# A recurrence and a highway layer from a hand-written list of operations: halves of output products for the last units, and a new list

## The chip, the cores and the metric

The kernel runs on one core of one Trainium2 chip. The metric is device time in microseconds. The engines are called as in the profile: PE (TensorE, matrix products and transposes), PEld (its weight loads), DVE (VectorE), ACT (ScalarE), POOL (GpSimd) and SP (the queue that issues the transfers). PSUM is the memory that PE writes to and from which DVE and ACT read.

## The reference

Two layers in a row over four sequences of 6336 tokens with 256 features. The first is a gated recurrence along the tokens, the second a highway layer with two 256 x 256 weight matrices. All inputs and the output are float32.

```python
f = lower_bound + (1 - lower_bound) * sigmoid(f_logit)
h = f[:, t] * h + (1 - f[:, t]) * x[:, t]          # for each token t; y[:, t] = h
H = maximum(y @ w_h, 0)
T = sigmoid(y @ w_t + b_t)
out = T * H + (1 - T) * y
```

## The kernel before, in words

The 25344 tokens are cut into 28 units: units 0 and 1 of 2 blocks of 128 tokens, unit 2 of 4, units 3 to 25 of 8, unit 26 of 4, unit 27 of 2. Each unit goes through the same stages, and most stages have two parts, one for each half of the 256 features (or of the unit's tokens). A part is a token of a list that is written out by hand as a string, such as `z23.0:0`: the letter says the stage, 23 is the unit, 0 the part, and the number behind the colon is the buffer (slot) that the result takes. A `v` at the end puts the work on DVE where another engine is the default. The stages:

- `l`, `x` (line 237, SP): load the logits and the inputs, 1 MB each for a full unit. `wt`, `wh` load the weights.
- `u` (line 249, ACT): sigmoid of the negated logits. `b` (line 257, POOL, `v` DVE): bv = u * x.
- `i` (line 264, PE): transposes u, features on partitions. `f` (line 275 ACT, line 273 DVE with `v`): the gate f from it.
- `p` (line 284, PE): transposes bv. `s` (line 301, DVE): the scan along the tokens, y; it needs the last column of the unit before.
- `z`, `g` (lines 114 and 313, PE): products of both halves of y with w_t and w_h. `t` (line 326, ACT): sigmoid of z. `d` (line 330, DVE): max of -(1 - lower_bound) * y and g, by which the rectified part minus y comes out. `e` (line 336, POOL, `v` DVE): d = d * t.
- `o` (lines 355 and 356, PE): sums y and d back to token order in PSUM, four blocks of 128 tokens at a time. `c` (line 368 ACT, line 366 DVE with `v`): copy to SBUF. `w` (line 372, SP): store, 512 KB for four blocks.
- `k` (lines 125 and 114, PE): `k*3` is three products of zeros that keep PE working.

PSUM has eight banks. Slots 0, 1 and 2 of `z`, `g`, `o` and `k` hold two banks each (`two_banks`, line 134); slots `a0` and `a1` are one bank each, and shared with the transposes `i` and `p`. A PE operation that takes a slot waits until its last reader is done.

The program keeps the order of the list on every engine: each engine's queue is the list with the other engines' tokens left out, and an engine never passes a waiting operation. The SP queue holds loads and stores in list order too, so a load behind a store waits for that store's copy. One more rule: a POOL product waits for the last DVE product of the same kind listed ahead of it (`shared`, line 178).

`part` (line 341) says how many blocks an `o` and its `c` cover, and a store waits for all copies of its four blocks:

Of the kernel before, what the change touches and what calls it, by code (L numbers as in the profile page):

```python
# [53 lines left out]
s3.1:0 c1.0:1 w1.0 x6:1 b4.1:1 l7:0 z2.0:2 p3.0:1 i4.0:0 t2.1:0 g2.0:0 s3.0 g2.1:1 d2.0:0 b4.0 x27:2 t2.0 k*3:2 f4.0:0
x7:3 e2.0 d2.1 e2.1 i4.1:0 u5:1 p4.0:1 f4.1:1 z3.0:0 b5.1:0 z3.1:1 t3.0:1 b5.0 t3.1 p4.1:0 k*3:2 s4.0:1 u6:0 u27:2
s4.1 g3.1:0 g3.0:1 i5.1:1 d3.1:1 f5.1:0 i5.0:0 e3.2 l8:2 o2.0:2 d3.0 e3.0v c2.0:0 f5.0:1 g4.1:0 e3.1v x8:5 i6.1:1
b6.1:1 g4.0:1 d4.1:0 d4.0 f6.1:2 o3.0:2 i6.0:0 p5.0:1 s5.0:2 o3.1:0 c3.0:1 f6.0:3 c3.1:2 b6.0 z4.0:1 w3.1 w3.0 p5.1:0
w2.0 z4.1:2 k*3:0 l9:1 s5.1 p6.0:1 u7:1 t4.1:0 x9:0 t4.0 s6.0:0 b27.0:2 l11:0 k*3:0 b7.0:0 x11:1 z5.0:0 l10:3 x10:2
t5.0:1 p6.1:0 g5.1:2 b7.1 e4.1 s6.1 z5.1:1 i7.0:1 d5.1:1 u8:0 f7.0:0 t5.1 k*3:0 g5.0:0 d5.0 i8.1:0 i7.1:1 b8.1:1
z6.0:2 e4.0v e4.2v f8.1:1 f7.1:2 p7.0:0 g6.0:0 e5.0v e5.2v e5.1v t6.0:0 i8.0:1 f8.0:3 b8.0 o4.1:1 d6.0:2 o5.0:2 e6.0  # L60
c4.1:0 p7.1:1 u9:1 c5.0:1 k*3:0 s7.0:3 o4.0:0 w5.0 c4.0:2 w4.1 b9.1:0 w4.0 z6.1:1 b9.0 t6.1 i9.0:0 g6.1:2 s7.1 f9.0v:0
d6.1 l12:1 z7.1:0 i9.1:1 p8.1:0 s8.1:1 e6.1 u11:0 f9.1:2 g7.1:1 k*3:2 t7.1:1 e6.2 i11.1:1 p8.0:0 x12:3 b11.1:3 o5.1:0
l13:2 d7.1:0 s8.0 f11.1:1 g7.0:1 z7.0:2 u10:1 i10.1:1 c5.1:3 b11.0 p9.0:0 t7.0 d7.0 s9.0:2 f10.1:3 o6.0:0 b10.1:1
g8.1:1 w5.1 b10.0 i10.0:1 c6.0:1 f10.0:0 z8.0:2 p9.1:0 d8.1:1 o6.1:0 t8.0:0 c6.1:0 w6.1 u12:1 e7.0 g8.0:1 p10.0:1
x13:0 s9.1 d8.0 z8.1:2 i11.0:0 z9.0:0 k*3:1 f11.0:2 t9.0:2 b12.1:0 l14:0 s10.0:0 t8.1 p10.1:0 s10.1 o7.0:1 c7.0:2
u13:0 w7.0 g9.1:0 p11.1:1 x14:1 l17:1 g9.0:2 w6.0 d9.1:2 l15:3 i12.0:0 o7.1:1 f12.0:0 c7.1:0 d9.0 z10.1:0 z10.0:2
p11.0:0 t10.1:1 z9.1:1 t10.0 s11.1:3 g10.0:0 w7.1 s11.0 i12.1:1 g10.1:2 e8.0 t9.1 x15:2 d10.0:0 d10.1 f12.1:1 b12.0
o8.1:1 i13.1:0 u14:1 f13.1:2 b13.1:1 o8.0:0 c8.1:2 p12.1:1 b13.0 z11.1:2 i13.0:0 t11.1:0 c8.0:3 e9.0v e10.0 g11.1:1
# [5 lines left out]
b16.1 g14.1:0 i16.0:0 t13.1 f16.0:2 e13.0 b17.1:3 s15.0:3 z14.1:1 t14.1:1 o12.0:2 p15.1:0 g14.0:1 d14.1:1 b17.0
c12.0:2 w12.0 p16.0:1 u18:3 s15.1 z14.0:0 t14.0 x19:0 d14.0 o12.1:2 e14.0 c12.1:3 i16.1:0 f16.1:1 z15.0:1 t15.0:0
g15.1:0 o13.0:2 w12.1 c13.0:0 b18.0:0 s16.0:1 p16.1:0 d15.1:2 w13.0 l20:1 i17.1:1 l21:2 x20:1 g15.0:0 s16.1 b18.1
o13.1:1 f17.1:2 d15.0 p17.0:1 p17.1:0 u19:0 s17.1:2 c13.1:1 z16.1:2 t16.1:2 s17.0 z15.1:0 w13.1 o14.0:1 t15.1 z16.0:2
i18.0:0 g16.1:0 c14.0:2 g16.0:1 i18.1:1 w14.0 t16.0 f18.0:1 o14.1:2 f18.1:0 d16.1:0 d16.0 z17.0:0 c14.1:0 x21:3 w14.1
# [5 lines left out]
t19.1:1 t19.0 g19.1:1 b22.0 d19.1 i21.0:0 w17.0 g20.1:0 d20.1:1 o18.0:2 p21.0:1 f21.0:2 u23:1 s21.0:2 p21.1:0 o18.1:1
z20.0:0 c18.0:2 l24:0 e19.0 g20.0:2 c18.1:0 w18.0 i22.1:1 z20.1:1 s21.1 t20.0:0 o19.1:0 f22.1:2 b23.0:1 x24:0 d20.0
p22.1:0 s22.1:0 t20.1 c19.1:3 i23.1:1 o19.0:1 g21.1:0 f23.1:0 d21.1:0 i23.0:1 c19.0:1 p22.0:0 b23.1 g21.0:1 w18.1
u24:0 f23.0:2 s22.0 d21.0 z21.0:0 t21.0:1 z21.1:2 i24.0:1 f24.0:1 t21.1 p23.1:0 s23.1:3 z22.1:0 g22.1:1 w19.1 i24.1:1
# [2 lines left out]
l26:2 o21.0:0 w20.1 c21.1:2 i25.0:1 g23.0:2 i25.1:0 c21.0:3 f25.0:0 b25.0 d23.0 f25.1:1 g24.1:0 z24.0:1 u26:0 i27.1:0  # L90
p25.0:1 z23.1:2 e22.0 f27.1:2 e22.2 x26:0 d24.1:0 o22.0:0 e23.0 p25.1:0 s25.0:2 t24.0:1 o22.1:1 w20.0 s25.1 t23.1
z24.1:2 c22.0:0 g24.0:0 c22.1:1 d24.0 e23.2 i26.0:1 g25.0:1 d25.0:2 t24.1 i27.0:0 b26.1:0 g25.1:2 f26.0:0 f27.0:1
d25.1 i26.1:1 b26.0 z25.0:0 w21.1 f26.1:3 p26.1:0 o23.1:1 s26.1:0 t25.0:2 e23.1 p26.0:1 e24.0 s26.0 o23.0:2 p27.1:0
# [4 lines left out]
"""

    NU = len(units)  # L100
# [57 lines left out]
    cc = sb([P, NH], FP32, "cc")  # L158
# [180 lines left out]
        return q * 4, min(q * 4 + 4, units[n][0])  # L339

    def part(n, k):
        w = 2 if n in () else 4
        return k * w, min(k * w + w, units[n][0])

    def do_o(n, k, eng, slot):
        op = two_banks(slot, "op").rearrange("p (j d) -> p j d", d=D)
        a, c = part(n, k)
        j0, j1 = blocks(n, a // 4)
        g = j1 - j0
        for j in range(a, c):  # L350
            lo = j0 * P + j - j0
            cols = slice(lo, lo + g * (P - 1) + 1, g)
            for h in range(NH):
                o = op[:, j - a, h * P:(h + 1) * P]
# [1 line left out]
                pin(nc.tensor.matmul(o, half(n, "d", h)[:, cols], ident_b, start=False, stop=True))  # L356
        st[n]["op", k] = op

    def do_c(n, k, eng, slot):
        a, c = part(n, k)  # L360
# [4 lines left out]
        if eng:
            pin(nc.vector.tensor_copy(to, of))
        else:
            pin(nc.scalar.copy(to, of))  # L368
# [44 lines left out]
```

## Time and profile before

| what | us |
| --- | --- |
| median of three runs | 208.80 |
| lowest and highest run | 208.68, 209.03 |
| the profiled execution | 208.92 |
| its span, first to last instruction | 207.1 |
| PE, DVE, ACT, POOL busy | 196.7, 193.0, 191.8, 176.9 |

The profile lists busy times for each engine, groups of equal instructions with a count, a mean in ns and the idle time ahead of them with what ended it, and stretches of the span. In rows of a timeline the first number is the start, the second the duration, and a bracket gives the idle time of the engine just before it and what ended it. The granted clock of PE was 0.994 of full speed over the span.

### The profile page before, as it was taken

The page shows a single profiled execution, that of the slowest core. Times are in us where ns is not written, and L with a number is a line of the kernel's source. Part 1 is how long each engine was busy: PE and PEld are TensorE (multiplying, and loading weights), DVE is VectorE, ACT ScalarE, POOL GpSimd, SP SyncE. Part 2 cuts the span into 40 slices and gives each one's busy share as a digit, 9 for nine tenths or more (in the row PEclk, how much of TensorE's full clock was granted, in tenths as well). Part 3 has the DMA queues.
Part 4 walks back from the last instruction along what each step waited for, and adds up shares of the span by engine and source line. Part 5 has one row for each costly group of instructions (what it writes and reads, how often), then busy time and mean ns, then how long its engine had stood idle before and what let it go on. Part 6 is the DMA issues. An engine that isn't in the chain of part 4 may idle for free.

```text
span 207.1 us, 4655 instructions
## 1 busy us (share of the span) xinstructions
PE 196.7 (95%) x1835; PEld 136.3 (66%) x1864; DVE 193.0 (93%) x157; ACT 191.8 (93%) x187; POOL 176.9 (85%) x94
## 2 busy tenths in 40 slices
...
GB/s 194 386 426 419 419 416 418 415 401 426 419 414 418 422 430 416 413 421 394 354 418 420 415 418 426 415 422 422 422 426 415 323 422 370 337 136 203 186 297 279
DMA packets 15980, 78.67 MB, mean 380 GB/s; under 512 B 1748, under 2 KB 2264, under 8 KB 10072
## 3 DMA queue, kind: packets, MB, share of 16 engines
...
q14 instruction: 6, 0.05, 0.1%
q10 hardware_dynamic: 8, 0.00, 0.0%
...
## 4 chain that ended last, share of the span: by engine, by line
PE 71%; DVE 10%; DMA 9%; issue 3%; ACT 2%; POOL 2%; SPq 0%; ACTq 0%; DVEq 0%; POOLq 0%
PE z L313 9%; PE g L313 9%; PE op L356 9%; PE op L355 9%; PE bT L284 9%; PE uT L264 8%; PE g L114 8%; PE z L114 7%; DVE y L301 7%; DMA x<-in_x_dram 7%; DMA l<-in_f_logit_dram 2%; DVE d L330 2%; POOL bv L257 2%; PE idle L114 1%; DVE d L336 1%
## 5 line engine op out<-in xcount | busy, mean ns | idle before, releaser
L257 POOL TENSOR_TENSOR bv<-u,x 128x1024 bf16<-128x1024 f16 (+1 forms) x51 | 103.1, 2049 | 14.1 <-DVE d L336 6.0
L301 DVE TENSOR_TENSOR_SCAN y<-f,y,bT 128x1024 bf16<-128x1024 f16 (+5 forms) x54 | 106.2, 1989 | 0.3 <-PE bT L284 0.2
L336 POOL TENSOR_TENSOR d<-d,t 128x512 bf16<-128x512 bf16 (+3 forms) x32 | 74.0, 2322 | 10.7 <-DVE d L336 4.1
L330 DVE SCALAR_TENSOR_TENSOR d<-y,ncc,g 128x1024 bf16<-128x1024 bf16 (+2 forms) x56 | 62.8, 1139 | 2.2 <-PE g L313 2.1
L326 ACT ACTIVATE t<-z,bt 128x1024 bf16<-128x1024 f32 (+2 forms) x56 | 57.3, 1058 | 1.6 <-PE z L313 1.0
L275 ACT ACTIVATE f<-uT,ncc 128x1024 f16<-128x1024 f16 (+2 forms) x51 | 53.8, 1065 | 2.7 <-PE uT L264 2.2
L249 ACT ACTIVATE u<-l 128x2048 f16<-128x2048 f32 (+2 forms) x28 | 48.9, 1753 | 4.8 <-DMA l<-in_f_logit_dram 4.8
L368 ACT COPY o<-op 128x1024 f32<-128x1024 f32 (+1 forms) x50 | 50.8, 1027 | 1.9 <-PE op L356 1.6
L355 PE MATMUL op<-diag,y 128*128 128x128 f16 x396 | 49.8, 219 | 0.8 <-DVE d L330 0.6
L356 PE MATMUL op<-ident_b,d 128*128 128x128 bf16 x396 | 49.5, 219 | 0.2 <-DVE d L336 0.2
L356 PEld LDWEIGHTS <-d 128*128 128x128 bf16 x396 | 44.0, 113 | 5.2 <-DVE d L336 1.1
L355 PEld LDWEIGHTS <-y 128*128 128x128 bf16 x396 | 44.2, 113 | 3.1
L313 PE MATMUL g<-y,w_sb 128*128 128x512 bf16 (+1 forms) x111 | 39.1, 367 | 1.0 <-ACT t L326 0.2
L313 PE MATMUL z<-y,w_sb 128*128 128x512 bf16 (+1 forms) x108 | 38.0, 367 | 0.7
L264 PEld LDWEIGHTS <-u 128*128 128x128 f16 x396 | 26.3, 98 | 11.4 <-issue 3.0
L284 PE MATMUL bT<-ident_f,bv 128*128 128x128 f32 x198 | 31.2, 276 | 1.7 <-DVE y L301 1.1
L114 PE MATMUL g<-y,w_sb 128*128 128x512 bf16 x84 | 31.8, 379 | 0.1
L264 PE MATMUL uT<-ident_h,u 128*128 128x128 f16 x396 | 30.8, 220 | 0.7 <-DVE y L301 0.3
L313 PEld LDWEIGHTS <-w_sb 128*128 128x128 f16 x224 | 21.5, 98 | 14.7 <-issue 0.3
L114 PE MATMUL z<-y,w_sb 128*128 128x512 bf16 x79 | 29.9, 379 | 0.2
L284 PEld LDWEIGHTS bT<-ident_f,bv 128*128 128x128 f32 x198 | 22.5, 141 | 8.7 <-DVE y L301 1.2
L114 PEld LDWEIGHTS <-w_sb 128*128 128x128 f16 x184 | 18.0, 98 | 15.5 <-issue 2.3
...
## 6 DMA issues: line engine op xcount, KB each, us to landing
...
x<-in_x_dram SPq DMA_DIRECT2D x23, 1024.0 KB, 12.0
...
```

Of the source, the lines that this page charges most:

```text
L114: return pe.add_instruction(mybir.InstMatmult(name=nc.get_next_instruction_name(), start_tensor_calc=start, stop_tensor_calc=stop, tile_si ...
L257: shared(pin(e.tensor_mul(st[n]["bv"][:, a:c].rearrange("p k d j -> p k j d"), st[n]["u"][:, 2 * a:2 * c].rearrange("p (k j) d -> p k j d" ...
L264: pin(nc.tensor.transpose(uT[:, j * P:(j + 1) * P], st[n]["u"][:, j, h * P:(h + 1) * P], ident_h))
L275: pin(nc.scalar.activation(to, of, AF.Identity, scale=ncc[:, h:h + 1], bias=1.0))
L284: pin(nc.tensor.transpose(words[:, k:k + g * (P - 1) + 1:g], pair, ident_f))
L301: pin(nc.vector.tensor_tensor_scan(y[:, c:e], st[n]["f", h][:, c:e], st[n]["bT", h][:, c:e], 0.0 if fresh else carry[h], op0=ALU.mult, op1 ...
L313: pin(nc.tensor.matmul(p[:, a:e], w, half(n, "y", ki)[:, a:e], start=ki == 0, stop=ki == NH - 1))
L326: pin(nc.scalar.activation(half(n, "t", m), st[n]["z", m][:, :tokens(n)], AF.Sigmoid, bias=bt[:, m:m + 1]))
L330: pin(nc.vector.scalar_tensor_tensor(half(n, "d", m), half(n, "y", m), ncc[:, m:m + 1], st[n]["g", m][:, :tokens(n)], op0=ALU.mult, op1=AL ...
L336: shared(pin(e.tensor_mul(st[n]["d"][:, a:c], st[n]["d"][:, a:c], st[n]["t"][:, a:c])), not eng)
L355: pin(nc.tensor.matmul(o, half(n, "y", h)[:, cols], diag[:, h], start=True, stop=False))
L356: pin(nc.tensor.matmul(o, half(n, "d", h)[:, cols], ident_b, start=False, stop=True))
```

## The change

Three things. First, `part` gives the `o` and `c` of units 24, 25 and 26 two blocks instead of four: an `o` there fills one bank, and so can take a one-bank slot (`o25.0:a0`) as well as a two-bank one. Units 24 and 25 have four such parts (o24.0 to o24.3), unit 26 two. The stores stay as they are. Second, the small `z` and `g` of units 1, 26 and 27 take slots of either size (`g1.1:a0`, `z26.0:1`, `g27.1:a1`); before, some of those of units 26 and 27 were in one-bank slots already. Third, the whole list is replaced by a new one: 824 tokens in place of 814. It holds the same stages, with other slots, another order on every queue, and some work on another engine: seven `f`, fourteen `e`, three `b` and four `c` have their `v` put or taken away, and of the five new `c` parts c25.2 has one. One output product, `o1.0*1`, has one more product of zeros ahead of it.

The first lines of the list, the lines around z23.0, its end, and `part`:

```diff
-l0:0 x0:0 l1:1 wt x1:1 l2:2 wh pc:0 u0:0 x2:2 k*3:1 cc l3:3 b0.0:0 u1:1 i0.0:0 x3:3 l4:0 f0.0:0 WT i0.1:1 x4:4 l5:4
-k*3:0 x5:0 k*3:0 p0.0:0 k*3:0 f0.1:1 dg p0.1:1 s0.0:0 i1.0:0 s0.1 l6:1 b1.0:1 f1.0v:0 l27:5 k*3:0 i1.1:1 z0.0:0 z0.1:1
-k*3:2 u2:0 t0.0:0 f1.1v:1 i2.0:0 k*3:0 WH i2.1:1 g0.1:0 d0.1:0 b2.1:0 f2.0:2 p1.0:0 g0.0:2 t0.1 f2.1:3 b2.0v e0.1
-k*3:1 p1.1:1 s1.0:1 s1.1 d0.0 k*3:0 p2.0:0 g1.0:0 e0.0 z1.1:1 p2.1:1 u3:1 d1.0:1 z1.0:2 t1.0:1 o0.0:0 s2.0:2 t1.1 s2.1
...
+l0:0 l1:1 x0:0 x1:1 l2:2 wh u0:0 wt pc:0 i0.1:0 x2:2 l3:3 x3:3 l4:0 x4:4 k*3:1 k*3:a1 l27:4 u1:1 i0.0:1 cc f0.0:0
+k*3:0 b0.0v:0 p0.1:1 dg f0.1:1 k*3:0 s0.1:0 p0.0:0 i1.1:1 f1.1:1 k*3:0 b1.0:1 s0.0 l5:1 k*3:0 p1.1:0 k*3:0 WH i1.0:1
+WT k*3:0 u2:0 s1.1:1 z0.0:0 p1.0:0 f1.0:0 g0.0:1 i2.0:1 t0.0:0 z0.1:2 f2.0:1 k*3:0 g0.1:0 t0.1 b2.0:0 s1.0 x5:5 i2.1:0
+d0.0:0 b2.1v d0.1 e0.1 k*3:a1 p2.1:1 f2.1v:0 z1.0:0 e0.0 g1.0:1 k*3:2 g1.1:a0 u3:1 o0.0:2 s2.1:2 p2.0:1 d1.0:1 b3.0:1
+c0.0:0 d1.1 t1.0:0 z1.1:1 t1.1 s2.0 b3.1v i3.0:0 w0.0 f3.0:0 u4:0 k*3:a1 g2.1:0 e1.0 i3.1:0 p3.0:1 l6:2 f3.1:1 e1.1
...
-t22.1:2 d22.1:2 z22.0:2 e20.0 b24.0:0 p23.0:0 s23.0 o20.1:0 l25:1 b24.1 e21.0 f24.1:3 g22.0:1 t22.0 d22.0 c20.1:0
-o20.0:2 p24.0:1 s24.0:1 z23.0:0 p24.1:0 w19.0 e22.1 x25:1 s24.1 u25:0 g23.1:1 c20.0:1 b25.1:0 o21.1:2 t23.0:0 d23.1:1
...
+z22.1:1 b24.1 u25:2 o20.0:0 i24.0:0 g22.1:2 t22.1:0 x26:0 f24.0:0 o20.1:1 c20.0:0 c20.1:1 i24.1:0 p24.0:1 d22.1
+z23.0:0 s24.0:1 g23.0:2 z22.0:1 f24.1:1 d23.0:0 e21.0 p24.1:0 x25:1 b25.1:1 t23.0:2 t22.0 i25.1:1 f25.1:0 s24.1 b25.0
...
-e24.2v e24.1 s27.1:3 z25.1:0 g26.0:a1 c23.1:2 w21.0 d26.0:1 o24.1:1 e25.0v w22.0 g26.1:a0 d26.1 c23.0:0 t25.1 e25.1v
-o24.0:0 c24.1:3 w22.1 w23.1 p27.0:1 z26.1:a0 s27.0 w23.0 o25.0:1 z26.0:a1 c24.0:1 t26.1:0 e25.2v t26.0 w24.1 z27.1:a0
-t27.1:1 o25.1:0 z27.0:a1 e26.1 g27.1:a0 w24.0 c25.0v:2 e26.0v c25.1:0 o26.0:1 d27.1:0 g27.0:a0 d27.0 w25.0 t27.0
-c26.0:3 e27.1 e27.0v o27.0:a0 c27.0:1 w25.1 w26.0 w27.0
...
+e25.2 c24.2:1 p27.0:0 c24.3 w23.0 c24.1:3 s27.0:3 z26.0:1 p27.1:1 o24.0:2 t26.0:1 c24.0 z26.1:0 s27.1 o25.0:a0 o25.1:1
+o25.3:2 g27.1:a1 e26.0 t26.1 z27.1:0 w23.1 c25.1:0 c25.0v o25.2:a0 z27.0:1 w24.1 d27.1:2 c25.3:2 e26.1 g27.0:a1
+o26.0:2 c25.2v d27.0 w24.0 w25.0 t27.1:0 o26.1:0 w25.1 t27.0 e27.1 c26.1:1 e27.0v o27.0:1 c26.0v w26.0 c27.0v:3 w27.0
 """
...
     def part(n, k):
-        w = 2 if n in () else 4
+        w = 2 if n in (24, 25, 26,) else 4
         return k * w, min(k * w + w, units[n][0])
```

More of the change, by code (lines that the diff above doesn't have):

```diff
@@ L54 @@
[L54 to L68, printed above, removed]
@@ L74 @@
[L74 to L78, printed above, removed]
@@ L84 @@
[L84 to L87, printed above, removed]
-t22.1:2 d22.1:2 z22.0:2 e20.0 b24.0:0 p23.0:0 s23.0 o20.1:0 l25:1 b24.1 e21.0 f24.1:3 g22.0:1 t22.0 d22.0 c20.1:0
@@ L89 @@
-o20.0:2 p24.0:1 s24.0:1 z23.0:0 p24.1:0 w19.0 e22.1 x25:1 s24.1 u25:0 g23.1:1 c20.0:1 b25.1:0 o21.1:2 t23.0:0 d23.1:1
[L90 to L93, printed above, removed]
@@ new lines @@
+x11:4 k*3:1 g6.1:1 z6.0:2 t6.1:2 t6.0 i9.0:0 b27.0:0 e5.0v e5.1v s7.0:3 f9.0:0 b8.1:2 e5.2v e4.0v p7.1:1 o5.1:0 d6.1:2
+c5.1:0 b8.0 w5.1 o4.1:2 x10:1 i8.0:0 c4.1:1 b9.1:1 f8.0:2 w4.1 g6.0:1 o4.0:0 s7.1 o5.0:2 c4.0:2 p8.0:0 c5.0:3 w4.0
+i8.1:1 l17:1 d6.0 k*3:0 e6.1v g7.1:0 w5.0 z7.1:1 f8.1:1 e6.2v s8.0:1 e6.0 l12:2 u11:0 b9.0 x12:2 p8.1:0 t7.1:0 i9.1:1
+f9.1:2 b11.1:2 g7.0:2 z7.0:1 b11.0 l13:4 d7.1:0 i11.1:1 u10:2 s8.1 f11.1:1 t7.0 d7.0 p9.0:0 s9.0:2 b10.0:3 z8.0:0
+g8.0:2 i10.1:1 p9.1:0 f10.1:3 x13:3 t8.0:1 b10.1 z8.1:1 i11.0:1 o6.0:0 d8.0:1 t8.1 g8.1:2 f11.0:0 s9.1 c6.0v:0 u17:0
@@ new lines @@
+c18.1:1 s21.1 z20.0:1 e19.0 z20.1:0 f22.1:1 x23:0 p22.1:1 l24:0 w18.0 d20.0 b23.1:1 i23.1:0 s22.1:0 g21.1:2 d21.1:1
+l25:2 x24:2 t20.0:0 t20.1 o19.1:1 f23.1:2 b23.0 p22.0:0 e20.0 s22.0 w17.0 u24:0 i23.0:1 z21.1:0 w18.1 c19.1:2 b24.0:2
+g21.0:2 t21.1:1 o19.0:1 d21.0 p23.1:0 f23.0:1 s23.1:3 z21.0:0 c19.0:3 p23.0:1 g22.0:2 d22.0:2 w19.1 s23.0 t21.0
+z22.1:1 b24.1 u25:2 o20.0:0 i24.0:0 g22.1:2 t22.1:0 x26:0 f24.0:0 o20.1:1 c20.0:0 c20.1:1 i24.1:0 p24.0:1 d22.1
+z23.0:0 s24.0:1 g23.0:2 z22.0:1 f24.1:1 d23.0:0 e21.0 p24.1:0 x25:1 b25.1:1 t23.0:2 t22.0 i25.1:1 f25.1:0 s24.1 b25.0
```

42 lines of the change are left out of this document (31 added, 11 removed).

## The prediction

> **What bounds the kernel now.** I read the page's first line and busy shares first, then the chain, then the busy time in stretches of the span, because the shares alone do not say where the idle time lies.
>
> ```profile
> span 207.1 us, 4655 instructions
> PE 196.7 (95%) x1835; PEld 136.3 (66%) x1864; DVE 193.0 (93%) x157; ACT 191.8 (93%) x187; POOL 176.9 (85%) x94
> PE 71%; DVE 10%; DMA 9%; issue 3%; ACT 2%; POOL 2%; SPq 0%; ACTq 0%; DVEq 0%; POOLq 0%
> ```
>
> ```profile
> core 0: us, PE busy (x) PEld busy (x) DVE busy (x) ACT busy (x) POOL busy (x), PEclk, DMA share, GB/s
> 0.00:5.00 5.00, 3.81 (x10) 1.31 (x11) 0.27 (x1) 2.17 (x3) 2.35 (x12) 1.00 0.61 190
> 5.00:20.00 15.00, 14.45 (x99) 8.41 (x101) 11.79 (x28) 9.70 (x14) 6.22 (x6) 1.00 1.02 410
> 40.00:190.00 150.00, 146.38 (x1406) 103.46 (x1427) 149.72 (x99) 148.49 (x138) 143.51 (x62) 1.00 0.98 395
> 190.00:199.00 9.00, 8.95 (x106) 7.03 (x107) 8.73 (x13) 7.43 (x9) 5.11 (x4) 1.00 0.43 169
> 199.00:207.10 8.10, 3.71 (x49) 3.02 (x48) 2.80 (x5) 4.00 (x7) 1.84 (x2) 0.85 0.77 301
> ```
>
> Between 40 and 190 us DVE is idle for 0.28 us and ACT for 1.51 of 150: both are full, PE nearly so, and the chain runs 71% through PE. DVE's 14.1 idle us lie at the two ends: 4.73 + 3.21 before 20 us and 5.57 after 190. So there is no slack in the middle to win, only slack to lose: a new order can gain at the start, in the tail, and through less work; and any place where one full engine is made to stand costs about its length. The profiled execution took 208.92 us for its 207.1 us span; the median of the three runs is 208.80. My sum is made against 208.92 and then lowered by 0.12.
>
> **Work that changes hands.** The prices are the rows of each shape:
>
> ```profile
> L368 ACT COPY o<-op 128x1024 f32<-128x1024 f32 x47 | 49.0, 1055 | 1.2 <-PE op L356 0.9
> L368 ACT COPY o<-op 128x512 f32<-128x512 f32 x3 | 1.8, 586 | 0.7 <-PE op L356 0.7
> L275 ACT ACTIVATE f<-uT,ncc 128x1024 f16<-128x1024 f16 x43 | 49.3, 1155 | 1.2 <-PE uT L264 0.7 <-DVE y L301 0.2
> L275 ACT ACTIVATE f<-uT,ncc 128x512 f16<-128x512 f16 x4 | 2.8, 688 | 1.2 <-PE uT L264 1.2
> L275 ACT ACTIVATE f<-uT,ncc 128x256 f16<-128x256 f16 x4 | 1.8, 475 | 0.3 <-PE uT L264 0.3
> L273 DVE TENSOR_SCALAR f<-uT,ncc 128x1024 f16<-128x1024 f16 x3 | 3.8, 1273 | 0.1
> L273 DVE TENSOR_SCALAR f<-uT,ncc 128x256 f16<-128x256 f16 x2 | 0.9, 472 | 0.0
> L366 DVE COPY o<-op 128x1024 f32<-128x1024 f32 x1 | 1.2, 1224 | 0.3 <-PE op L356 0.3
> L330 DVE SCALAR_TENSOR_TENSOR d<-y,ncc,g 128x512 bf16<-128x512 bf16 x4 | 2.8, 730 | 0.0
> L257 DVE TENSOR_TENSOR bv<-u,x 128x512 bf16<-128x512 f16 x1 | 0.7, 728 | 0.0
> L336 DVE TENSOR_TENSOR d<-d,t 128x512 bf16<-128x512 bf16 x8 | 3.3, 420 | 0.0
> L336 DVE TENSOR_TENSOR d<-d,t 128x256 bf16<-128x256 bf16 x2 | 0.6, 292 | 0.1
> L336 POOL TENSOR_TENSOR d<-d,t 128x512 bf16<-128x512 bf16 x12 | 13.9, 1166 | 4.4 <-ACT t L326 3.0 <-DVE d L336 1.0 <-DVE d L330 0.4
> ```
>
> DVE gives up three full and two 256-wide forget gates (3 x 1.27 + 2 x 0.47 = 4.8 us) and takes two 512-wide ones (estimate 0.74 each, between 0.47 and 1.27): 1.5. It takes one more full copy (1.22), four copies of halves (estimate 0.70 each: 1.22 halved, plus about a tenth for the fixed part) and one more 512-wide bv (0.73), and gives up two d products (0.42 and 0.29). Sum: +0.8 us.
> ACT loses six full copies (6.33) and two 512-wide gates (1.38), and gets six half copies (3.52), three full gates (3.47) and two 256-wide ones (0.95): +0.2. The split alone costs 2 x 586 - 1055 = 117 ns for each copy that is cut in two, six of them 0.7 us. The Trainium skill's page Perfetto Trace Analysis, section Optimizing Scalar/DVE Operations, puts the fixed part of a ScalarE operation on PSUM at about 51 ns; by that figure the six would cost 0.3 us and ACT would come out at -0.2. The row here is for this very copy, so it decides, and the sum keeps +0.2.
> POOL gives up one 512-wide bv and takes one 512-wide and one 256-wide d product: about +0.7, bounded by 0 and 1.2, in an engine that is idle 3.9 of 9 us from 190 on: I take nothing. PE gets one zero matmul, 0.22 us at most; the halves of the output products have as many matmuls as before. DMA moves the same bytes in as many transfers.
> DVE was full, so if nothing else moved the 0.8 would be paid whole. It is not all paid: see the tail.
>
> **The start.** x0 is now the third transfer and not the second, wt the seventh and not the fourth.
>
> ```profile
> 4.27 1.17 POOL L257 TENSOR_TENSOR bv<-u,x 128x512 bf16<-128x512 f16 x1 [2.02 <-DMA x<-in_x_dram]
> 6.53 0.63 ACT L249 ACTIVATE u<-l 128x512 f16<-128x512 f32 x1 [2.45 <-DMA l<-in_f_logit_dram]
> 13.77 1.91 ACT L249 ACTIVATE u<-l 128x2048 f16<-128x2048 f32 x1 [0.34 <-DMA l<-in_f_logit_dram]
> 17.06 0.59 ACT L368 COPY o<-op 128x512 f32<-128x512 f32 x1
> 18.08 1.11 ACT L275 ACTIVATE f<-uT,ncc 128x1024 f16<-128x1024 f16 x1 [0.43 <-PE uT L264]
> 20.28 2.35 DVE L301 TENSOR_TENSOR_SCAN y<-f,y,bT 128x1024 bf16<-128x1024 f16 x1
> ```
>
> The second transfer was there at 4.2, the third at 6.5. So l1 comes 2.3 us earlier, x0 as much later, and the first product, now on DVE, runs at 6.5. Laying the listed operations end to end from there with the rows' durations, I get the first scan of unit 3 at 21.05 instead of 20.28; but DVE has by then done about 0.9 us more of its work (a 512-wide bv, gate and max more, 0.73 + 0.74 + 0.73; two 256-wide gates and a d product fewer, 0.94 + 0.29), so it stands 0.1 us better, and 0.3 better by unit 4, where the same laying out finds no wait for the second scan of unit 3. Bounds: 0 to 0.5; I take 0.3.
> ACT stands worse. The gates of unit 1 now run on it ahead of u3, which starts at about 14.2 instead of 13.8, and the copy c0.0 has been put ahead of t1.0 and t1.1: it must wait for e0.1, e0.0 and o0.0, to 17.05, so ACT idles a microsecond that it did not (before, those two sigmoids ran from 16.3). The first gate of unit 3 starts at 18.45 instead of 18.08 with 0.15 us more done. Worked on to unit 5 the lag is 0.2 to 0.55; I take 0.3, near the lower end, because part of the 0.55 is that mean durations run slow against this stretch. Nothing behind it gives it back: ACT is full from 20 us on.
>
> **The middle: what is late next.** PE works in list order and waits where a PSUM slot is not yet read out. I compared, for each product, the work listed ahead of it on PE with the work listed ahead of the reader that frees its slot. Up to unit 22 the new list is about as tight as the old. The sharpest change is at z23.0, which now takes the slot that o20.0 left, and so waits for the copy c20.0; before, it followed o20.1 and c20.1.
>
> ```profile
> 171.34 1.13 ACT L275 ACTIVATE f<-uT,ncc 128x1024 f16<-128x1024 f16 x1
> 172.33 1.13 ACT L326 ACTIVATE t<-z,bt 128x1024 bf16<-128x1024 f32 x1
> 173.33 1.04 ACT L368 COPY o<-op 128x1024 f32<-128x1024 f32 x1
> 174.23 1.95 ACT L249 ACTIVATE u<-l 128x2048 f16<-128x2048 f32 x1
> 176.04 1.04 ACT L368 COPY o<-op 128x1024 f32<-128x1024 f32 x1
> 175.15 0.38 PE L313 MATMUL z<-y,w_sb 128*128 128x512 bf16 x1
> 175.37 0.38 PE L114 MATMUL z<-y,w_sb 128*128 128x512 bf16 x1
> ```
>
> Before, c20.1 ended at 174.37 and z23.0 ran at 175.15, unhindered, 0.8 us later. In the new list u25 and its neighbours have been moved ahead of c20.0. Counted to the copy's end, ACT has one u more (start to start 1.81), two full gates more (0.99 each), two 256-wide more (0.95), and one sigmoid (1.00), two copies (0.90 each) and one 512-wide gate (0.69) fewer: +1.25. With the start's 0.3 the copy ends at 174.37 + 1.25 + 0.3 = 175.9, so z23.0 starts at 175.95, 0.8 us later than before. And PE has by then one z less behind it (four matmuls, 0.22 apart: 0.87), with nothing else changed in the count. PE is thus 1.65 us behind. Below, it is behind by 0.9 if ACT has picked up 0.75 on the way (its idle 40 to 190 us is 1.51, so not more than half of it); above, by 2.2, if ACT stands the 0.5 later and the scans, each waiting for its transposes on PE, push DVE and ACT further. What is behind the waiting product: p24, the z, g and o of units 22 to 27, and through p24 to p27 DVE's scans; they are all later by it.
> The loads: 512 KB more lie ahead of x24 and l26, 1.25 us at the 400-odd GB/s of the windows, and x26 lands earlier. x24 makes POOL stand about 1 us before b24.0; POOL's slack from 190 on covers it, and if it did not, the 1 us would be added.
>
> **The tail.** From 190 on PE was full and DVE and ACT waited on it:
>
> ```profile
> 198.72 0.81 PE L313 MATMUL z<-y,w_sb 128*128 128x512 bf16 x3
> 200.97 0.48 DVE L330 SCALAR_TENSOR_TENSOR d<-y,ncc,g 128x256 bf16<-128x256 bf16 x1 [0.43 <-PE g L313]
> 202.02 0.48 DVE L330 SCALAR_TENSOR_TENSOR d<-y,ncc,g 128x256 bf16<-128x256 bf16 x1 [0.56 <-PE g L313]
> 201.84 1.01 ACT L368 COPY o<-op 128x1024 f32<-128x1024 f32 x1
> 203.60 0.59 ACT L368 COPY o<-op 128x512 f32<-128x512 f32 x1 [0.74 <-PE op L356]
> ```
>
> From 198.72 both lists have 3.5 us of matmuls left on PE. With PE standing as before, DVE in the new list does c25.0, d27.1, c25.2, d27.0, e27.0 and c26.0 after o25.0 (0.70 + 0.44 + 0.70 + 0.44 + 0.25 + 0.70 = 3.2), with some 0.6 of waits for g27.1 and o25.2: c26.0 ends at about 202.8, and before at 201.84 + 1.01 = 202.85. c27.0 would end near 203.5 instead of 204.19, but its store is issued right behind the 512 KB one of unit 26, so I credit 0.1. The half copies thus pay for DVE's extra 0.8 us by filling its waits (0.43 + 0.56), and the tail itself gives nothing. A lag of PE goes through, less what was waiting in it: PE's last product stood about 0.5 for e27.0 before.
>
> **Sum.** Work 0 (hidden in the tail's waits), DVE's start 0 (PE decides), PE's lag at z23.0 +1.65, its recovered wait and the credit -0.4: +1.25. 208.92 + 1.25 - 0.12 = 210.05; I say 210.0.
>
> **Rivals.**
> Faster: z23.0 finds its slot free (c20.0 done before 175.1, which needs ACT 0.8 earlier than I reckon), so PE stands as before, and the halves let ACT and DVE read out at once. The two 0.4 to 0.6 waits of DVE and ACT's 0.74 before the last copy go, up to 1.3 together; half of it gives 208.2, all of it 207.5. For it: ACT and DVE are idle half of the last 8 us. Against it: those waits are for PE, which is full until 200. It decides from the point where PE's lag falls under 0.4. The Trainium skill speaks for this case in the same section of Perfetto Trace Analysis: breaking up instructions may allow work to be completed sooner where ScalarE and VectorE are not saturated but cause bubbles on other engines. Here the bubbles were theirs, not PE's, which is why I keep it a rival.
> No change: ACT regains its 0.3 and PE half of its lag, and the tail the rest: 208.8 plus or minus 0.4.
> Much slower: the lag at z23.0 and x24's microsecond add up because POOL's e24 products, needed by four halves in the tail, come late: 211.5.
>
> **How the numbers follow.** Forecast (PE late by 0.8 to 2.2 at the end, 209.3 to 211.2): 0.58. Faster: 0.28. No change: 0.08. Much slower: 0.06. The measurement tells 0.2%, 0.4 us, from no change. Slower is 0.64, same 0.08, faster 0.28. The range leaves out 0.05 to 0.1 at either side: 208.1 to 211.2; the likeliest case's own is 209.3 to 211.2.
>
> **What would show it.** Right: ACT's c0.0 waiting a microsecond for PE op near 16 to 17 us; z23.0 starting after 175.6, released by ACT's copy; DVE waits for bT or g between 175 and 200 that were not there; DVE busy 193.8; the last copy ending after 205. Wrong: DVE idle under 0.5 us from 40 to 199, z23.0 before 175.2, or a last copy before 204. The weakest step is ACT's place at 174 us: the lag carried over 150 us rests on a start worked out by hand.

## The result and the profile after

The changed kernel takes 211.14 us, median of seven runs (209.81 to 213.28; the highest was disturbed and is left out of the ratio), against 208.84 us before (208.67 to 209.06). The ratio is 1.009, 95% interval 1.0068 to 1.0112: 1.4 to 2.3 us slower. The profiled execution took 210.64 us for a span of 208.8, 1.7 us more than the span of before.

The page's first lines and its chain, then busy time in the same stretches as before:

```profile
span 208.8 us, 4689 instructions
PE 199.6 (96%) x1865; PEld 136.6 (65%) x1865; DVE 193.9 (93%) x158; ACT 191.0 (91%) x190; POOL 177.5 (85%) x95
PE 58%; ACT 21%; issue 7%; DVE 6%; POOL 4%; DMA 2%; ACTq 0%; DVEq 0%; POOLq 0%
```

```profile
core 0: us, PE busy (x) PEld busy (x) DVE busy (x) ACT busy (x) POOL busy (x), PEclk, DMA share, GB/s
0.00:5.00 5.00, 3.81 (x11) 1.29 (x12) 0.27 (x1) 2.79 (x4) 1.62 (x11) 1.00 0.61 197
5.00:20.00 15.00, 14.07 (x89) 7.71 (x90) 11.18 (x26) 7.48 (x13) 5.74 (x5) 1.00 1.02 406
20.00:40.00 20.00, 19.68 (x175) 13.16 (x175) 19.32 (x14) 19.98 (x20) 17.49 (x12) 1.00 0.98 396
40.00:190.00 150.00, 148.05 (x1425) 103.22 (x1423) 149.46 (x100) 149.44 (x138) 141.74 (x60) 1.00 0.97 391
190.00:199.00 9.00, 8.74 (x99) 6.54 (x98) 9.00 (x12) 6.70 (x9) 7.39 (x6) 1.00 0.57 226
199.00:208.80 9.80, 5.29 (x76) 4.66 (x74) 4.65 (x9) 4.61 (x9) 3.56 (x4) 0.98 0.76 300
```

Between 40 and 190 us DVE is the engine with the least idle time in both kernels (0.28 and 0.54 us; ACT has 1.51 and 0.56, so in the changed kernel the two are equally full). I split its span into work and idle time per stretch (a stretch's length less DVE's busy time; the page gives the work). The last two columns are experiments that follow below.

| DVE, us | before | changed | old list, late start | new list, one zero group less |
| --- | --- | --- | --- | --- |
| work | 193.0 | 193.9 | 193.0 | 194.1 |
| idle 0 to 40 | 8.25 | 9.23 | 9.74 | 7.72 |
| idle 40 to 190 | 0.28 | 0.54 | 0.31 | 1.13 |
| idle 190 to 199 | 0.27 | 0.00 | 0.00 | 0.00 |
| idle from 199 | 5.30 | 5.15 | 5.57 | 4.85 |
| span | 207.1 | 208.8 | 208.6 | 207.8 |

The 1.7 us are 0.9 of work and 1.0 of idle time at the start, 0.3 more in the middle, less 0.4 at the end. The start is where the profile says most. DVE, ACT and PE there:

```profile
8.83 1.37 DVE L301 TENSOR_TENSOR_SCAN y<-f,bT 128x256 bf16<-128x256 f16 x2 [1.80 <-PE bT L284]
13.73 0.75 DVE L301 TENSOR_TENSOR_SCAN y<-f,y,bT 128x256 bf16<-128x256 f16 x1 [1.41 <-PE bT L284]
22.43 2.35 DVE L301 TENSOR_TENSOR_SCAN y<-f,y,bT 128x1024 bf16<-128x1024 f16 x1
7.86 0.84 ACT L275 ACTIVATE f<-uT,ncc 128x256 f16<-128x256 f16 x2 [3.28 <-PE uT L264]
18.58 0.59 ACT L368 COPY o<-op 128x512 f32<-128x512 f32 x1 [1.63 <-PE op L356]
19.79 1.12 ACT L275 ACTIVATE f<-uT,ncc 128x1024 f16<-128x1024 f16 x1
5.09 0.63 PE L125 MATMUL idle<-zeros 128*128 128x512 bf16 x1
5.52 1.06 PE L114 MATMUL idle<-zeros 128*128 128x512 bf16 x2
6.37 0.63 PE L125 MATMUL idle<-zeros 128*128 128x512 bf16 x1
6.80 0.70 PE L114 MATMUL idle<-zeros 128*128 128x512 bf16 x2
7.55 0.27 PE L264 MATMUL uT<-ident_h,u 128*128 128x128 f16 x2
```

The third row is the first scan of unit 3: 22.43, where before it stood at 20.28. The first gate waits 3.28 us for the transposes i0.0 (last row, 7.55), and ahead of those PE works through `k*3:1 k*3:a1`, six products of zeros, for nearly 2.5 us. The fifth row is c0.0, and the sixth the first gate of unit 3, which before stood at 18.08.

The middle and the tail, at the places the prediction named:

```profile
174.58 2.08 ACT L368 COPY o<-op 128x1024 f32<-128x1024 f32 x2
175.81 0.38 PE L313 MATMUL z<-y,w_sb 128*128 128x512 bf16 x1
203.75 0.59 ACT L368 COPY o<-op 128x512 f32<-128x512 f32 x1 [0.68 <-PE op L356]
203.83 1.44 DVE L366 COPY o<-op 128x512 f32<-128x512 f32 x2
```

The first row holds c20.0, which ends at 175.76, and c20.1; z23.0 starts at 175.81, and the last copy ends at 205.27 (204.19 before). The list of waits from 165 us on gives z23.0's own wait; its columns are us in total, times, longest:

```profile
PE z L313 <- ACT o L368: 0.3, 1, 0.3
```

From the last copy to the end it is 3.53 us, before 2.91. The stretches of the last microseconds show why, of before first and then of the changed kernel (the column before the last is the DMA share):

```profile
205.00:206.00 1.00, 0.00 (x0) 0.00 (x0) 0.00 (x0) 0.00 (x0) 0.00 (x0) 0.50 0.72 266
206.00:207.00 1.00, 0.00 (x0) 0.00 (x0) 0.00 (x0) 0.00 (x0) 0.00 (x0) 0.50 0.00 0
```

```profile
205.00:206.00 1.00, 0.00 (x0) 0.00 (x0) 0.27 (x1) 0.00 (x0) 0.00 (x0) 1.00 0.95 369
206.00:207.00 1.00, 0.00 (x0) 0.00 (x0) 0.00 (x0) 0.00 (x0) 0.00 (x0) 1.00 0.99 387
207.00:208.00 1.00, 0.00 (x0) 0.00 (x0) 0.00 (x0) 0.00 (x0) 0.00 (x0) 1.00 0.42 158
```

The stores drain until 207.4 in place of 205.7. In the new list c26.0, the copy that releases unit 26's 512 KB store, is the last but one and ends only 0.76 us ahead of the last; before, it ended 1.34 us ahead. In two other profiles below the same numbers go together too: 1.33 us ahead and 2.9 us to the end with the late start in the old list, 0.43 us ahead and 3.8 us to the end where units 25 and 26 are whole.

### The profile page after: what moved, and what is told of

Read it like the earlier page. It is cut to its first block, busy times and chain, and to the rows that moved or that the text cites. A ratio compares the mean times of both kernels' runs of the same rounds, so it can differ in the third digit from the quotient of the medians.

```text
span 208.8 us, 4689 instructions
## 1 busy us (share of the span) xinstructions
PE 199.6 (96%) x1865; PEld 136.6 (65%) x1865; DVE 193.9 (93%) x158; ACT 191.0 (91%) x190; POOL 177.5 (85%) x95
## 4 chain that ended last, share of the span: by engine, by line
PE 58%; ACT 21%; issue 7%; DVE 6%; POOL 4%; DMA 2%; ACTq 0%; DVEq 0%; POOLq 0%
PE uT L264 7%; PE z L313 7%; PE bT L284 7%; ACT f L275 7%; PE g L313 7%; PE op L356 6%; PE op L355 6%; ACT o L368 6%; PE g L114 5%; PE z L114 5%; ACT t L326 5%; PE idle L114 4%; DVE y L301 3%; ACT u L249 3%; PE idle L125 2%
## 5 line engine op out<-in xcount | busy, mean ns | idle before, releaser
L257 POOL TENSOR_TENSOR bv<-u,x 128x1024 bf16<-128x1024 f16 (+1 forms) x50 | 101.9, 2065 | 15.0 <-DVE ndiag L205 4.9
L336 POOL TENSOR_TENSOR d<-d,t 128x512 bf16<-128x512 bf16 (+3 forms) x34 | 75.7, 2240 | 10.2 <-DVE d L336 3.9
L275 ACT ACTIVATE f<-uT,ncc 128x1024 f16<-128x1024 f16 (+2 forms) x54 | 60.8, 1128 | 5.9 <-PE uT L264 5.5
L326 ACT ACTIVATE t<-z,bt 128x1024 bf16<-128x1024 f32 (+2 forms) x56 | 59.9, 1119 | 1.3 <-PE z L313 0.7
L368 ACT COPY o<-op 128x1024 f32<-128x1024 f32 (+1 forms) x50 | 49.0, 1033 | 4.3 <-PE op L356 3.4
L249 ACT ACTIVATE u<-l 128x2048 f16<-128x2048 f32 (+2 forms) x28 | 50.5, 1806 | 0.5 <-DMA l<-in_f_logit_dram 0.5
L313 PE MATMUL z<-y,w_sb 128*128 128x512 bf16 (+1 forms) x112 | 39.5, 367 | 0.7 <-ACT o L368 0.6
L114 PE MATMUL z<-y,w_sb 128*128 128x512 bf16 x92 | 34.9, 379 | 0.0
L114 PE MATMUL g<-y,w_sb 128*128 128x512 bf16 x92 | 34.8, 379 | 0.0
L284 PE MATMUL bT<-ident_f,bv 128*128 128x128 f32 x198 | 31.9, 278 | 1.1 <-DVE y L301 0.5
```

What stands on the lines that cost most here:

```text
L114: return pe.add_instruction(mybir.InstMatmult(name=nc.get_next_instruction_name(), start_tensor_calc=start, stop_tensor_calc=stop, tile_si ...
L257: shared(pin(e.tensor_mul(st[n]["bv"][:, a:c].rearrange("p k d j -> p k j d"), st[n]["u"][:, 2 * a:2 * c].rearrange("p (k j) d -> p k j d" ...
L275: pin(nc.scalar.activation(to, of, AF.Identity, scale=ncc[:, h:h + 1], bias=1.0))
L284: pin(nc.tensor.transpose(words[:, k:k + g * (P - 1) + 1:g], pair, ident_f))
L313: pin(nc.tensor.matmul(p[:, a:e], w, half(n, "y", ki)[:, a:e], start=ki == 0, stop=ki == NH - 1))
L326: pin(nc.scalar.activation(half(n, "t", m), st[n]["z", m][:, :tokens(n)], AF.Sigmoid, bias=bt[:, m:m + 1]))
```

## The experiments

The theory on record, M: PE is made late at z23.0 by the copy c20.0, and the start is worth little. The rival that the trace suggests, S: the start makes DVE late, and as DVE is full from 20 to 199 us it stays late. What remains is then the work moved to DVE, and the tail. Ratios are to the kernel before, run beside each. The diffs show the tokens around each change, taken out of the list's longer lines; `...` stands for what is left out between them.

### A late start in the old list

```diff
-f0.1:1 dg p0.1:1 s0.0:0
+f0.1:1 dg k*3:1 k*3:1 k*3:1 p0.1:1 s0.0:0
```

> The kernel before with nine more zero products (three groups of three, they feed nothing of the result) ahead of the transposes p0.1 at about 8 us, and nothing else changed: a late start put into the old list. Nine at 0.22 us are 1.9 us of PE, part of it in time that PE had free. Theory S (DVE is full from 20 to 199 us, so what the start loses is lost at the end): DVE's first scan of unit 3 comes 1.2 to 1.7 us later than at 20.28, and the time rises by 1.0 to 1.6 us, ratio 1.005 to 1.008. Rival G (a late start is given back in the middle, because PE and ACT then wait less): the scan is as late, the time rises by 0.6 us at most, ratio up to 1.003.

Measured: 210.95 us, ratio 1.0081 (1.0057 to 1.0105), 1.2 to 2.2 us more. The first scan of unit 3:

```profile
21.78 2.35 DVE L301 TENSOR_TENSOR_SCAN y<-f,y,bT 128x1024 bf16<-128x1024 f16 x1
```

It is 1.50 us late, and the profiled span is 1.5 us longer. In the table DVE's idle time grows by 1.49 before 40 us and by 0.03 between 40 and 190. The net delay of 1.50 us is carried whole, and rival G falls for delays.

### An early start in the new list

One group of three zero products less, and i0.0 ahead of the other:

```diff
-x4:4 k*3:1 k*3:a1 l27:4 u1:1 i0.0:1
+x4:4 i0.0:1 k*3:1 l27:4 u1:1
```

> The changed kernel with i0.0 moved ahead of the zero products at about 5 us, and one of the two groups of three zero products there left out (it feeds nothing of the result). In the changed kernel's trace these groups run from 5.1 to 7.5 us ahead of i0.0, and the gate f0.0 waits 3.28 us for i0.0, to 7.86. Theory S, in its narrow form (these zeros are what makes the start late): f0.0 starts at about 6.5, the first scan of unit 3 about 1 us earlier (21.4), and the time falls by 0.7 to 1.2 us: ratio 1.003 to 1.006. S in its wider form (the order of unit 1 and the copy c0.0 ahead of t1.0 make it late too, so DVE waits for PE again behind the first scan): 0.2 to 0.6 us less. Theory M: within 0.3 us of the changed kernel.

The same, with all zeros kept:

```diff
-x4:4 k*3:1 k*3:a1 l27:4 u1:1 i0.0:1
+x4:4 i0.0:1 k*3:1 k*3:2 l27:4 u1:1
```

> The changed kernel with i0.0 moved ahead of the two groups of zero products, as in the run with one group left out, but with both groups kept (the second in another slot). If it was the order that made the start late (f0.0 waited for i0.0 to 7.86 us): f0.0 starts at about 5.6, the first scan of unit 3 is 0.7 us or more earlier than 22.43, and the time is 0.4 to 0.8 us less than the changed kernel's. If it was the amount (six zero products at 0.22 to 0.43 us each stand ahead of everything that follows on PE, p0.1 and p0.0 too): f0.0 is early, but the first scan of unit 3 moves by 0.4 us at most and the time by 0.2.

Measured: 210.40 us, ratio 1.0062 (1.0031 to 1.0093), and 210.19 us, ratio 1.0053 (1.0026 to 1.0081). The first scans of unit 3, in a row that holds both scans, of the one and of the other:

```profile
21.00 4.58 DVE L301 TENSOR_TENSOR_SCAN y<-f,y,bT 128x1024 bf16<-128x1024 f16 x2
```

```profile
21.08 4.58 DVE L301 TENSOR_TENSOR_SCAN y<-f,y,bT 128x1024 bf16<-128x1024 f16 x2
```

Both stand where the prediction had laid the changed kernel's own scan, at 21.05. That is not the order's doing alone. In the second run's profile the zeros are 0.22 us apart from the first on, in the changed kernel's 0.43 apart until about 6.8 (see the last section). The kernel with all units whole, further down, has the changed kernel's start and the quick zeros:

```profile
21.45 4.58 DVE L301 TENSOR_TENSOR_SCAN y<-f,y,bT 128x1024 bf16<-128x1024 f16 x2
```

Between profiles with quick zeros the order is thus worth 0.37 us (21.45 to 21.08), and the rate of the zeros is worth 0.98 (22.43 to 21.45). What the order alone is worth with slow zeros no run shows: in the first run they are slow until 6.36, but there are three fewer. The time falls, by less than the 1.4 us: the three kernels with the new start as it is have 1.0090, 1.0105 and 1.0105 (two follow), these two 1.0062 and 1.0053, so 0.6 to 1.1 us. Each interval alone overlaps that of the changed kernel. The two together lie below the three by 0.9 us, about 0.35 to 1.4; this takes the edits of the other two as neutral. In the table the early start wins 1.51 us by 40 us and gives 0.59 back between 40 and 190, where DVE then stands idle for others. M, which allowed 0.3, hardly fits; S does in sign, and in 0.4 to 0.8 of its size.

### Old start with new rest, and new start with old rest

```diff
-l0:0 l1:1 x0:0 x1:1 l2:2 wh u0:0 wt pc:0 i0.1:0 x2:2 l3:3
...
+l0:0 x0:0 l1:1 wt x1:1 l2:2 wh pc:0 u0:0 x2:2 k*3:1 cc l3:3
...
+d2.0:0 b4.0 x27:5 t2.0 k*3:2 d2.1 u27:1 f4.0:0 x7:2 u5:2
```

> The first 115 tokens of the list of before (to about unit 4, 29 us of the span), then the new list's remaining tokens in the new order; x27 takes an input buffer that neither list needs at that time. Theory S (the start decides): the trace of the changed kernel shows the first scan of unit 3 at 22.43 us, of before at 20.28, and DVE's idle time summed up to 31 us at about 9.65 in place of 8.3; DVE is full from there to 198 us, so the 1.35 us is carried to the end. With the old start it goes: 1.0 to 1.4 us less than the changed kernel, ratio to before 1.002 to 1.005. Theory M (the one on record: PE's wait at z23.0 for the copy c20.0, and the lag behind it): the start is worth 0.3 at most, the ratio stays between 1.007 and 1.010.

```diff
-z2.1:1 d2.1:0 t2.1:0 b4.1:0 s3.0:0 o1.0*1:0 u27:1 c1.0:1
+z2.1:1 d2.1:0 t2.1:0 p3.1:0 o1.0:1 s3.1:0 c1.0:1
```

> The counterpart: the first 100 tokens of the new list (to about unit 4), then the remaining tokens of before in the order of before, without halves. Theory S: DVE's first scan of unit 3 comes at about 22.4 us and its idle time by 31 us is about 1.35 us more than before; ratio 1.005 to 1.007, 209.9 to 210.2 us where before takes 208.8. Theory M: the start costs 0 to 0.3 us, ratio 0.999 to 1.0015.

Measured: 219.57 us, ratio 1.0424 (1.0365 to 1.0483), and 213.55 us, ratio 1.0215 (1.0186 to 1.0243). Neither tells anything about S or M: the seams cost far more than the effect sought. In the first, ACT reaches u27, which the new list has early, while the old list's loads bring its logits late:

```profile
30.09 0.63 ACT L249 ACTIVATE u<-l 128x512 f16<-128x512 f32 x1 [6.57 <-DMA l<-in_f_logit_dram]
```

In the second, from 18 to 45 us, the scans wait 4.0 us for transposes. Here two lists that are good each could not be cut and joined without a cost.

### The copy c20.0 earlier

```diff
-u25:2 o20.0:0 i24.0:0 g22.1:2 t22.1:0
+o20.0:0 c20.0:0 u25:2 i24.0:0 g22.1:2 t22.1:0
...
-o20.1:1 c20.0:0 c20.1:1 i24.1:0
+o20.1:1 c20.1:1 i24.1:0
```

> The changed kernel with the copy c20.0 moved ahead of u25 on ACT, right behind o20.0, so that the slot of z23.0 is free about 1.5 us earlier (in the changed kernel's trace c20.0 runs from 174.58 to 175.76 and z23.0 starts at 175.81). Theory M: z23.0 starts between 174.3 and 175.0, PE is 1.0 to 1.5 us ahead, the last copy ends as much earlier, and the time falls by 0.7 to 1.3 us, ratio 1.003 to 1.006. Theory S: z23.0 starts earlier, but DVE is full and its place does not move; the time changes by no more than 0.3 us either way, ratio 1.0075 to 1.0105.

```diff
-u25:2 o20.0:0 i24.0:0
+o20.0:0 i24.0:0
...
-c20.1:1 i24.1:0
+c20.1:1 u25:2 i24.1:0
```

> The changed kernel with u25 on ACT put back behind the copies c20.0 and c20.1 (the prediction named u25, moved ahead of c20.0, as what makes z23.0 late). Theory M (on record): c20.0 ends 1.8 us earlier, z23.0 starts 0.7 to 1.5 us earlier than its 175.81, PE's lag is gone by as much and the time falls by 0.5 to 1.3 us, ratio 1.003 to 1.0065. Theory S: z23.0 starts earlier and nothing is won, because z23.0 waited only 0.3 us for the copy in the changed kernel's trace; the late u25 makes unit 25's gates and products late, so 0 to 0.8 us more, ratio 1.009 to 1.013.

Measured: 215.30 us, ratio 1.0294 (1.0255 to 1.0333), and 211.25 us, ratio 1.0105 (1.0078 to 1.0131). Both theories missed the first. ACT and PE show what it did (the last two rows are z23.0's first products):

```profile
172.61 1.01 ACT L368 COPY o<-op 128x1024 f32<-128x1024 f32 x1 [1.68 <-PE op L356]
173.51 1.91 ACT L249 ACTIVATE u<-l 128x2048 f16<-128x2048 f32 x1
175.33 1.11 ACT L326 ACTIVATE t<-z,bt 128x1024 bf16<-128x1024 f32 x1
176.48 0.22 PE L355 MATMUL op<-diag,y 128*128 128x128 f16 x1 [2.60 <-ACT t L326]
179.15 0.63 PE L313 MATMUL z<-y,w_sb 128*128 128x512 bf16 x1
179.57 0.63 PE L114 MATMUL z<-y,w_sb 128*128 128x512 bf16 x1
```

The copy now waits 1.68 us for o20.0; u25 and t22.1 queue behind it; and o20.1, which takes t22.1's slot, holds PE for 2.60 us. Behind that wait PE's products run 0.42 us apart until 180.85 and 0.22 apart again from 181.09 on; the granted clock from 178 to 180 us is 0.50. So the wait costs more than its own length. The new list has u25 just there as work for ACT until o20.0 is done. In the second, u25 goes behind both copies, and ACT is no earlier for it:

```profile
172.07 1.11 ACT L326 ACTIVATE t<-z,bt 128x1024 bf16<-128x1024 f32 x1 [0.74 <-PE z L114]
174.36 1.92 ACT L368 COPY o<-op 128x1024 f32<-128x1024 f32 x2
175.35 0.61 PE L284 MATMUL bT<-ident_f,bv 128*128 128x128 f32 x4
175.79 0.81 PE L313 MATMUL z<-y,w_sb 128*128 128x512 bf16 x2
```

With 1.8 us of u taken out ahead of it, the copy starts 0.22 us earlier (ACT waits for z22.1 instead), z23.0 at 175.79 in place of 175.81, and the time stays. Neither edit brought z23.0 forward, so neither prices an earlier z23.0. What speaks against M is PE's own row: p24.0, the transposes right ahead of z23.0 on PE, start at 175.35 in this kernel (third row) and in the changed one alike, and z23.0 follows 0.44 and 0.46 us behind them. PE came there late of itself. Of a lag of 1.65 us the copy made 0.3 at most, and M is refuted in that.

### Halves

All of units 24 to 26 whole, and everything from the 689th token on ordered anew for the slots that this needs. Fourteen `e`, `f` and `c` go to another engine by it, and not the three that the expectation names:

```diff
-        w = 2 if n in (24, 25, 26,) else 4
+        w = 2 if n in () else 4
...
-o24.2:1 d26.1 o24.3:2 o24.1:0 e25.1v
+e24.2v g25.1:2 o24.1:0 d26.0:0 d25.1 g26.1:a0 c24.1:1
```

> The changed kernel with the output products of units 24 to 26 whole again. As whole ones need slots of two banks at other times, the last 110 tokens are ordered anew for them, and three gates or e products change their engine; everything ahead is the new list. Theory H (the halves earn their split cost and more in the last 10 us): 0.4 to 1.0 us more than the changed kernel, ratio 1.011 to 1.014. The step on record (the halves pay for DVE's extra work in the tail and give nothing more): without them DVE has two copies of 0.70 less and the tail has its old waits of 0.4 to 0.7 back; within 0.3 us of the changed kernel, ratio 1.0075 to 1.0105.

Units 25 and 26 whole in the new list, all else in place:

```diff
-        w = 2 if n in (24, 25, 26,) else 4
+        w = 2 if n in (24,) else 4
...
-s27.1 o25.0:a0 o25.1:1 o25.3:2 g27.1:a1 e26.0 t26.1 z27.1:0 w23.1 c25.1:0 c25.0v o25.2:a0 z27.0:1 w24.1 d27.1:2 c25.3:2
+o25.0:1 s27.1 o25.1:2 g27.1:a1 e26.0 t26.1 z27.1:0 c25.0v:0 w23.1 z27.0:1 w24.1 c25.1:2 d27.1:2
...
-e26.1 g27.0:a1 o26.0:2 c25.2v d27.0 w24.0 w25.0 t27.1:0 o26.1:0 w25.1 t27.0 e27.1 c26.1:1 e27.0v o27.0:1 c26.0v w26.0
+e26.1 g27.0:a1 o26.0:2 d27.0 w24.0 w25.0 t27.1:0 w25.1 t27.0 e27.1 c26.0:1 e27.0v o27.0:1 w26.0
```

> The changed kernel with the output products of units 25 and 26 whole again, at the places of their first halves: o25.0 and o25.1 in slots of two banks, c25.0 on DVE, c25.1 and c26.0 on ACT, and every other token where it was. Unlike the run with all halves undone, nothing else is re-ordered. Step on record (the halves only pay for the extra work, the tail gives nothing): DVE has three half copies of 0.69 less and one whole of 1.2 more, ACT two whole ones for two halves; within 0.3 us of the changed kernel, ratio 1.0075 to 1.0105. Theory H (the halves let both engines read out while PE is still writing, so the last unit's products and its store come earlier): 0.5 to 1.2 us more than the changed kernel, ratio 1.0115 to 1.015.

Halves of units 25 and 26 in the old list:

```diff
-        w = 2 if n in () else 4
+        w = 2 if n in (25, 26,) else 4
...
-o25.0:1 z26.0:a1 c24.0:1
+o25.0:1 z26.0:a1 o25.1:2 c24.0:1
...
-o25.1:0 z27.0:a1 e26.1 g27.1:a0 w24.0 c25.0v:2 e26.0v c25.1:0 o26.0:1
+o25.2:0 z27.0:a1 e26.1 g27.1:a0 w24.0 c25.0v:2 c25.1v o25.3:2 e26.0v c25.2:0 c25.3 o26.0:1 o26.1:0
...
-c26.0:3 e27.1
+c26.0:3 c26.1 e27.1
```

> The counterpart: the list of before with the output products of units 25 and 26 in halves, each second half as near behind its first as a free slot lets it, copies on the engines they had; nothing else changes. Three copies are cut: 0.12 us more on ACT for each of two, about 0.16 on DVE for one. Theory H in its strong form (halves are worth half a microsecond anywhere): 0.3 to 0.8 us less than before, ratio 0.996 to 0.9985. The step on record (they earn their cost and no more): within 0.3 us, ratio 0.9985 to 1.0015.

Measured: 214.18 us, ratio 1.0243 (1.0196 to 1.029); 211.30 us, ratio 1.0105 (1.0075 to 1.0134); 209.54 us, ratio 1.0022 (1.0004 to 1.0039). The first is inconclusive: its new tail put an e product of DVE ahead of POOL's, and POOL waited,

```profile
POOL d L336 <- DVE d L336: 4.2, 2, 3.6
```

so it prices that order and not the halves. The second is the clean one, at the upper edge of what the step on record expects: without halves nothing is won and 0.3 us or so may be lost; the interval also reaches into theory H's range, from 1.0115 on. In the third halves alone cost 0.1 to 0.8 us, outside H's range. So no gain of theirs is seen in either list, and in the new one a small gain isn't excluded.

### Work on DVE

One full copy in the middle of the old list moved to DVE, and one 512-wide product at the start moved off it:

```diff
-i18.0:0 g16.1:0 c14.0:2 g16.0:1
+i18.0:0 g16.1:0 c14.0v:2 g16.0:1
```

> The kernel before with one copy in the full stretch, c14.0 at about 113 us, on DVE in place of ACT (the new list has two such copies there, c6.0 and c14.0): DVE gets 1.22 us more, ACT 1.05 less, nothing else. Theory S (in the middle DVE's own work sets the pace, so DVE's extra work in the new list is paid in full): 1.0 to 1.5 us more, ratio 1.005 to 1.007. Rival B (ACT is as full as DVE, so work moved from one to the other is neutral): within 0.3 us of before.

```diff
-f2.1:3 b2.0v e0.1
+f2.1:3 b2.0 e0.1
```

> The kernel before with one product, b2.0, on POOL in place of DVE, nothing else. It takes 0.73 us of DVE (its row in the profile of before) and about 1.17 on POOL, which is busy 6.2 of 15 us between 5 and 20. Theory S: DVE's 0.73 us before the first scan of unit 3 are gained and carried through: 0.4 to 0.7 us less, ratio 0.9965 to 0.998. Rival G: the gain is lost again where DVE then waits for PE or ACT; within 0.2 us of before.

Measured: 209.95 us, ratio 1.0050 (1.0029 to 1.0070), and 209.29 us, ratio 1.0008 (0.9985 to 1.0032). A copy of 1.22 us costs 0.6 to 1.5 us where DVE is full, though ACT has 1.05 less: work moved to DVE is paid. By that the 0.9 us of DVE's extra work cost about 0.8, an estimate (0.9 times 1.05 over 1.22, where 1.05 is the middle of 0.6 to 1.5). Taking 0.73 us off DVE at the start wins nothing that can be measured; as in the new list with the early start, a gain there isn't kept.

## Why the prediction was right and wrong

**The sum and its side.** Slower by 1.25 was the forecast, by 1.9 it came out. The terms were other ones.

**DVE's work, +0.8:** measured +0.9. "It is not all paid: see the tail" was wrong by the runs: the copy moved to DVE in the old list cost nearly its length.

**ACT's work, +0.2:** measured 0.8 less (191.0 for 191.8). I took the price of a cut copy, 117 ns, from mean durations, which reach into the next instruction. From start to start three halves in a row take (1.57 - 0.61) / 2 = 0.48 us each,

```profile
197.90 1.57 ACT L368 COPY o<-op 128x512 f32<-128x512 f32 x3 [0.89 <-DMA out_dram<-o]
```

and a whole copy 0.90 (173.33 to 174.23 in the prediction's rows): 2 x 0.48 - 0.90 = 0.06 us. That is near the 51 ns which the Trainium skill's page Perfetto Trace Analysis gives in Optimizing Scalar/DVE Operations, and which I had set aside for the row. With 0.06 for 0.117 on six copies the forecast would have been -0.1; the other 0.7 us of the gap I have not traced.

**The start, DVE 0.3 better:** this step failed. "PE gets one zero matmul, 0.22 us at most" counted the zeros, and neither their place ahead of i0.0 nor their rate. The scan I put at 21.05 came at 22.43. Of these 1.4 us 1.0 goes with zeros that run 0.43 apart instead of 0.22 (21.45 with quick ones), and 0.4 is left for their place; with i0.0 ahead of them it came at 21.00 and 21.08. In place of 0.3 won, 1.0 us was lost by 40 us. That c0.0 would make ACT idle about a microsecond was right: 1.63 us, to 18.58. But ACT's first gate of unit 3, put at 18.45, came at 19.79.

**"Nothing behind it gives it back":** half wrong. ACT is idle for 0.56 us between 40 and 190 where it had been for 1.51, so it picked up 0.95. DVE, idle 0.28 before, had nothing to pick up from, and its delay went through, as the late start in the old list shows.

**The middle:** the numbers were right by accident. The copy was to end at 175.9 and z23.0 to start at 175.95; they did at 175.76 and 175.81. ACT was 1.3 us later than forecast at the start and had made it up by then, and the product had waited 0.3 us at most. The failing step is that PE, but for the copy, was taken to stand where it stood before, at 175.15: it came to z23.0 at 175.8 of itself. Nor is ACT's place its sum of work where it waits for PE in between: with 1.8 us of u taken out ahead of the copy, the copy came 0.22 us earlier. The microsecond that POOL was to stand for x24, on which the much slower rival rests, isn't among POOL's waits from 20 us on.

**The tail gives nothing:** right for the halves as far as the runs tell, which show no gain of theirs. Sized wrongly was the store, which the prediction names: c26.0 late puts unit 26's 512 KB right ahead of the last store, and the end is 0.62 us further from the last copy than before. That the store does it is read from four profiles, not tested by an edit. "I credit 0.1" had the wrong sign.

**The rivals.** Faster needed z23.0's slot free and the halves to earn; neither mattered. Of what the prediction asked to see, nearly all was there (c0.0's wait, z23.0 after 175.6, DVE busy 193.9, a last copy after 205). Of new waits of DVE for transposes or g between 175 and 200 there was one, 0.28 us at 199.35; from 175 to 199 DVE is idle for 0.05 us. That row, and not the others, told M from S. The sign of being wrong that comes nearest is DVE idle under 0.5 us from 40 to 199: it was 0.54.

**The account.** Of 1.9 us the start is worth 0.6 to 1.1 by the repaired starts, DVE's work about 0.8 by the moved copy; both are estimates, and the first holds the rate of the zeros as well as their place. What is left is within the intervals. Why an early start isn't kept whole in the new list (0.59 us of new idle time between 40 and 190) stays open, and no version here beats the kernel before.
